# Queries and keys of batches 2 and 3 turned by the DMA crossbar instead of TensorE

## The chip, the cores and the metric

One core of one Trainium2 chip. The metric is the device time of one execution in microseconds (us); a profile of one execution gives its span, which is some 1.8 us shorter. Most executions agree within about 1%, but some are a few per cent longer ("slow": over 1.5% above the fastest of the same kernel). A ratio is the mean time of one kernel's fast runs over that of the kernel before in the same rounds on the same chip, with a 95% interval; it is therefore not quite the ratio of the medians quoted beside it.

## The reference, cut to what matters

```python
# q, k, v: (4 batches, 8 heads, 768 rows, 64), values 0.1 * normal
scores = q @ k.T / 8                       # keys kept: the 8 global rows, and 96 local ones
scores = where(keep, scores - slope[h] * dist, -1e9)
x = softmax(scores) @ v                    # heads side by side: (4, 768, 512)
x1, x2, x3 = split(x @ w_proj, 3)          # "gate" matmuls
y = x1 * irfft(rfft(x2) * rfft(filter)) * x3
out = y @ w_out                            # "output" matmuls, f32
```

Scores contract over the 64 values of a head, so TensorE needs queries and keys with these 64 on the partitions: each tile of 128 rows x 512 (8 heads x 64) has to be turned before its scores.

## The kernel before: the parts that the change touches

The program is first a graph of operations with estimated costs. A list scheduler lays it on the five engines' queues; its ranks come from a table of numbers (`NUDGES`) that was found by search for exactly this graph. Each queue is then run in order by the hardware.

Loads from HBM are issued by GpSimd (f32 to f16 on the way, 256-byte pieces in SBUF), a tile of 128 rows at a time, into one buffer `qn` (6 tiles) and one buffer `kn` (7 tiles), used by every batch in turn. A tile can be loaded again only when it has been turned. A key tile has 120 rows of its own and 8 rows for the global keys.

```python
    def transposes(self, what, t, src, cols):
        ...
            for i in range(4):                       # 4 x (128 x 128), f16, into one PSUM bank
                nc.tensor.transpose(b.f16()[:, P * i:P * i + P],
                                    src[:, 2 * i:2 * i + 2, :], self.ident)
        ...
        g.op("AV", ...copy of the bank into QT or KT, by ScalarE or VectorE...)
        if what == "k" and t == 0:                   # global key columns of all 7 tiles, by VectorE
            self.copy("V", kv[:, :, :, 0:NG], kv[:, :, 0:1, NG:2 * NG].to_broadcast([P, 4, 7, NG]))

    def load_global(self, vt, s):                    # global value rows, SBUF to SBUF, on SyncE
        for c, (t, n) in enumerate(((0, 2), (2, 5))):
            self.load("S", vt[0:NG, t:t + n], vt[NG:2 * NG, 0:1].to_broadcast(...), ...)

    def attention(self, b):                          # for b > 0, three groups c of rows
        for c in range(3):
            for t in ([0, 1, 2], [3, 4], [5])[c]:
                self.transposes("q", t, self.qn[:, t], P * t)
            for t in self.GRP[c]:                    # key tiles of the group: 0,1 / 2,3 / 4,5,6
                self.transposes("k", t, self.kn[:, t], P * t)
            for i in range(4):
                self.scores(i, c, ...)
            ...values, small transposes; gate matmuls of group c - 1...

    def fill(self, out):                             # idle matmuls where TensorE is planned to wait
        ...
            gap = o.start - at - 2.2 * (at < BEGIN + 1.0)
            n = int((gap - 0.1) / self.BUSY)
```

## Time and profile before

The median is 175.86 us. The profile is of another execution, of 177.28 us, and has a span of 175.5 us. What bounds it is read in the prediction below. Here are only lines of the page on its DMA queues. The first is a queue (packets, MB, packet time as a share of the 16 engines' span); the others are kinds of DMA with their size and the median us from issue to landing.

```profile
q1 hardware_dynamic: 4424, 7.30, 11.5%
...
vn<-in_v_dram POOLq DMA_DIRECT2D x28, 120.0 KB, 6.1
kn<-in_k_dram POOLq DMA_DIRECT2D x21, 120.0 KB, 6.0
qn<-in_q_dram POOLq DMA_DIRECT2D x18, 128.0 KB, 6.7
```

q1 is the queue of SyncE: 11.5% of 175.5 us is 20.2 us of the 16 engines, for the output, two loads of the first batch and the small copies. The loads are in another queue, q0.

| of the kernel before | us |
|---|---|
| first gate matmul starts | 27.0 |
| last scores of batch 1 / first of batch 2 / first of batch 3 | 60.6 / 72.5 / 117.3 |
| last output matmul starts | 171.4 |

These landmarks are start times in TensorE's timeline. From the first gate to the last output matmul TensorE works almost without a hole.

### The profile page before, as it was taken

The numbers are of one execution on the slowest core, as the hardware profiler recorded it, in microseconds if no ns is written. First come the engines' busy times: TensorE is split into PE (matmuls) and PEld (weight loads), VectorE is DVE, ScalarE is ACT, GpSimd is POOL, SyncE is SP. The second block draws the span as 40 slices with busy tenths as digits, with TensorE's granted clock in tenths as the row PEclk, the third lists the DMA queues.
The fourth block names the chain that finished last, engine by engine and source line by source line (L and its number), as shares of the span: only waits on it lengthen the run. The fifth ranks groups of instructions, "written<-read, shape, count | busy, mean of one in ns | idle before, by whom it ended". The sixth has DMA issues, their size and how long they took to land.

```text
span 175.5 us, 4566 instructions
## 1 busy us (share of the span) xinstructions
PE 166.9 (95%) x1768; PEld 104.3 (59%) x1768; DVE 157.0 (89%) x368; ACT 152.6 (87%) x304; POOL 75.3 (43%) x97
## 2 busy tenths in 40 slices
PE   7799999999899799999999999999999999999991
PEld 2357777665457567575446669754556674547540
DVE  6669778999999769999999998999899999998960
ACT  8879989999999778999997977999799897968751
POOL 7999986298997699998040300000000000000000
PEclk9999999999999999999999999999999999999998
DMA  5999999999999999999999900000710000043145
GB/s 177 148 145 134 146 200 209 166 152 138 135 166 159 132 141 142 146 144 149 66 63 344 70 4 4 0 0 0 294 70 4 0 2 4 0 159 140 60 166 197
DMA packets 79853, 20.06 MB, mean 114 GB/s; under 512 B 70528, under 2 KB 76888, under 8 KB 79832
## 3 DMA queue, kind: packets, MB, share of 16 engines
q0 software_dynamic: 75408, 12.47, 107.2%
q1 hardware_dynamic: 4424, 7.30, 11.5%
q8 instruction: 14, 0.23, 0.5%
q14 instruction: 7, 0.06, 0.1%
HBM read 25.69 MB, written 6.29 MB: 182 GB/s over the span
## 4 chain that ended last, share of the span: by engine, by line
PE 64%; DVE 14%; DMA 9%; POOL 5%; ACT 5%; issue 2%; ACTq 0%; POOLq 0%; DVEq 0%
PE bank L1098 19%; PE bank L1215 12%; DMA qn<-in_q_dram 9%; PE bank L1159 6%; PE bank L1181 4%; PE bank L1015 4%; PE bank L924 4%; PE bank L938 3%; PE bank L1020 3%; PE bank L975 3%; PE bank L1060 3%; ACT E L990 3%; POOL kn L583 2%; POOL vn L583 2%; PE bank L630 2%
## 5 line engine op out<-in xcount | busy, mean ns | idle before, releaser
L1098 PE MATMUL bank<-xT,w 128*128 128x384 f16 x256 | 45.6, 326 | 0.0
L990 ACT ACTIVATE E<-bank 128x864 f16<-128x864 f32 x48 | 41.0, 923 | 1.7 <-PE bank L975 1.3
L1098 PEld LDWEIGHTS <-w 128*128 128x128 f16 x256 | 23.9, 98 | 15.8 <-issue 0.8
L583 POOL DMA_DIRECT2D kn<-in_k_dram x24 | 21.6, 908 | 14.0 <-PE bank L938 6.6
L583 POOL DMA_DIRECT2D vn<-in_v_dram x29 | 26.2, 922 | 2.0 <-DMA w<-in_moe_w_proj_dram 1.6
L1215 PE MATMUL bank<-wo,y 128*128 128x512 f16 (+1 forms) x100 | 21.8, 371 | 0.1
L583 POOL DMA_DIRECT2D qn<-in_q_dram x21 | 18.6, 892 | 5.9 <-PE bank L755 3.2
L997 DVE TENSOR_TENSOR E<-E,mask 128x864 f16<-128x864 f16 x36 | 20.9, 597 | 0.1
L1039 DVE TENSOR_TENSOR xn<-bank,rc 128x512 f16<-128x512 f32 (+1 forms) x24 | 18.5, 775 | 0.4
L571 ACT ACTIVATE ot<-bank 128x512 f32<-128x512 f32 (+1 forms) x23 | 13.1, 606 | 5.1 <-PE bank L1215 5.0
L1108 ACT CAST g<-bank 128x384 f16<-128x384 f32 x32 | 15.7, 494 | 1.4 <-PE bank L1098 1.2
L1015 PEld LDWEIGHTS <-E 128*128 128x128 f16 x224 | 14.1, 97 | 3.6 <-DVE E L997 1.1
L571 ACT ACTIVATE ab<-bank 128x512 f16<-128x512 f32 x23 | 14.3, 633 | 2.2 <-PE bank L1159 2.0
L1215 PEld LDWEIGHTS <-y 128*128 128x128 f16 x100 | 9.5, 98 | 10.7 <-DVE y L1257 0.8
L1015 PE MATMUL bank<-vn,E 128*128 128x65 f16 x224 | 15.8, 194 | 0.0
L571 ACT ACTIVATE x<-bank 128x384 f16<-128x384 f32 x28 | 13.8, 507 | 2.3 <-PE bank L1098 1.8
L1020 PE MATMUL bank<-vn,E 128*128 128x65 f16 x192 | 15.4, 193 | 0.0
L975 PE MATMUL bank<-QT,KT 64*128 64x216 f16 (+2 forms) x224 | 15.0, 241 | 0.1
L1020 PEld LDWEIGHTS <-E 128*128 128x128 f16 x192 | 13.3, 97 | 0.4
L567 ACT CAST X<-bank 128x512 f16<-128x512 f32 x21 | 12.3, 643 | 0.0
L975 PEld LDWEIGHTS <-KT 64*128 64x128 f16 x224 | 8.3, 94 | 5.6 <-issue 3.0
L924 PE MATMUL bank<-ab,fwd 128*128 128x512 f16 x40 | 11.4, 379 | 0.0
(144 smaller groups left out, 358.2 us busy)
## 6 DMA issues: line engine op xcount, KB each, us to landing
out_dram<-ot SPq DMA_DIRECT2D x23, 256.0 KB
vn<-in_v_dram POOLq DMA_DIRECT2D x28, 120.0 KB, 6.1
kn<-in_k_dram POOLq DMA_DIRECT2D x21, 120.0 KB, 6.0
qn<-in_q_dram POOLq DMA_DIRECT2D x18, 128.0 KB, 6.7
w<-in_moe_w_proj_dram POOLq DMA_DIRECT2D x4, 256.0 KB, 7.3
g<-in_moe_filter_fft_dram POOLq DMA_DIRECT2D x1, 768.0 KB, 12.5
qn<-in_q_dram POOLq DMA_DIRECT2D x3, 192.0 KB, 5.0
kn<-in_k_dram POOLq DMA_DIRECT2D x3, 192.0 KB, 5.1
```

What stands on the lines that cost most here:

```text
L571: self.nc.scalar.mul(out, in_, c)
L583: return self.g.op(eng, 0.57 + 0.00035 * nbytes[0] if eng == "G" else 0.5, lambda _: e.dma_start(dst, src), w=w, r=r, nbytes=nbytes, name= ...
L924: self.nc.tensor.matmul(b.f32(), self.fwd[:, f], src(i, t), start=(n == 0), stop=(n == len(terms) - 1))
L975: nc.tensor.matmul(bs[hh].f32()[:, off:off + w], self.KT[hs, hp, P * m:P * m + P], self.QT[hs, hp, KL * m:KL * m + w], start=(off == 0 and ...
L990: g.op("A", act(864), lambda _: nc.scalar.activation(eo, bs[0].two()[:, :, 0:432].rearrange("p h (m w) -> p h m w", m=2), Act.Exp, scale=s ...
L997: g.op("V", dve(864, 2), lambda _: nc.vector.tensor_mul(eo, eo, mk), r=[("E", hp, gi), ("mask", hp)], w=[("E", hp, gi)], name="masked")
L1015: nc.tensor.matmul(o[:, n, hh], ef[:, at:at + P], vt[:, t, 2 * hp + hh, :], start=first, stop=(t == 0), skip_group_check=True)
L1020: nc.tensor.matmul(o[:, n, hh], ef[:, at:at + P], vt[:, t - 1, 2 * hp + hh, :], start=False, stop=True, skip_group_check=True)
L1039: nc.vector.tensor_mul(to, o[:, :, :, 0:D], rc.to_broadcast([P, 2, 2 * nt, D]))
L1098: nc.tensor.matmul(bk.f32()[:, 0:h], self.w[:, c, o + P * j:o + P * j + P], self.xT[:, c, h * s:h * s + h], start=(c == 0), stop=(c == 3))
L1108: g.op("A", act(h), lambda _: nc.scalar.copy(x3, pts[1].f32()[:, 0:h]), use=[pts[1]], w=[ko], name="x3")
L1215: nc.tensor.matmul(bk.f32()[:, 0:n], y[:, c, P * t:P * t + P], self.wo[:, c, cs], start=(c == 0), stop=(c == 3))
```

## The change

The intent: TensorE is the fullest engine, so the 104 transposes of batches 2 and 3, and the copies that follow them on ScalarE and VectorE, go to the DMA crossbar, whose result lands in QT and KT directly. As the crossbar turns all 128 rows, the global key rows have to be in each tile beforehand: SyncE copies them within `kn`, once the tiles of batch 1 have been turned. Some idle matmuls more keep TensorE's clock up in front.

```diff
+    CROSS = frozenset((b, w, t) for b in (2, 3) for w in "qk" for t in range(7))
...
+    def turned(self, b, what, t, src, cols):
+        if (b, what, t) not in self.CROSS:
+            self.transposes(what, t, src, cols)
+            return
+        dst = (self.QT if what == "q" else self.KT)[:, :, cols:cols + P]
+        keys = [("kng", min(t // 2, 1))] if what == "k" else []
+        self.g.op("S", 1.3, lambda _: self.nc.sync.dma_start_transpose(
+            out=dst, in_=src.rearrange("p h d -> p (h d)")), r=[(what + "n", t)] + keys,
+            w=[(what.upper() + "T", t)], nbytes=(512, 650), name=what + "T")
...
-    def load_global(self, vt, s):
+    def load_global(self, tile, key, *r):            # now for kn of batches 2 and 3 too
...
-                gap = o.start - at - 2.2 * (at < BEGIN + 1.0)
+                gap = o.start - at - 2.0 * (at < BEGIN + 1.0)
...
-    NUDGES = (...)      # 2112 numbers, now 2064, all new: the whole order is searched again
+    NUDGES = (...)
-    FAVOUR = 0.1
+    FAVOUR = 0.0
```

(The estimate for one load of the first batch was raised as well, 1536 to 1990.)

## The prediction

> **What bounds the kernel now.** I read the page's busy shares and forty slices first, to see which engine is full and where.
>
> ```profile
> PE 166.9 (95%) x1768; PEld 104.3 (59%) x1768; DVE 157.0 (89%) x368; ACT 152.6 (87%) x304; POOL 75.3 (43%) x97
> ...
> PE   7799999999899799999999999999999999999991
> ...
> DVE  6669778999999769999999998999899999998960
> ACT  8879989999999778999997977999799897968751
> ...
> DMA  5999999999999999999999900000710000043145
> ```
>
> The span is 175.5 us, so one slice is 4.4 us. TensorE is full from slice 14 (about 60 us) to the last; VectorE and ScalarE are nearly full as well, so three engines are close together, TensorE ahead. The DMA engines are 9 tenths full until about 88 us and almost empty afterwards: batches 2 and 3 are loaded in the first half. I then asked for the windows, to see whether "full" has holes.
>
> ```profile
> 27.00:60.00 33.00, 31.18 (x320) 19.41 (x317) 30.57 (x74) 31.00 (x58) 24.16 (x28) 1.00 2.33 158
> 112.00:171.00 59.00, 59.00 (x487) 33.96 (x486) 55.91 (x118) 50.62 (x99) 0.00 (x0) 1.00 0.17 66
> 27.00:171.00 144.00, 141.87 (x1379) 87.83 (x1376) 135.96 (x296) 128.11 (x244) 50.59 (x57) 1.00 1.11 103
> ```
>
> The columns are the window, its length, then busy us of PE, PEld, DVE, ACT and POOL, then clock, DMA share and GB/s. From the first gate matmuls (27 us) to the last output matmul (171 us) TensorE is idle for only 144.00 - 141.87 = 2.1 us, 1.8 of them before 60 us, and the clock is full. Thus work taken off TensorE after 27 us should come off the end nearly one for one, if nothing takes its place.
>
> Busy time of a matmul here includes its latency (219 ns for a transpose), so I take paces from the chain of waits, where the pieces are disjoint:
>
> ```profile
> PE 64%; DVE 14%; DMA 9%; POOL 5%; ACT 5%; issue 2%; ACTq 0%; POOLq 0%; DVEq 0%
> ...
> 49.13 9.36 DMA qn<-in_q_dram
> 58.54 0.40 PE bank L938 x4
> ...
> 109.61 1.12 PE bank L938 x20
> ...
> 111.06 0.89 PE bank L938 x16
> ```
>
> L938 is the transpose to be replaced: 0.89/16 and 1.12/20 us are 56 ns each. The chain also shows that at 58.5 us TensorE reached the first query tile of batch 2 before it had landed, 9.36 us after its issue. The waits confirm who suffers:
>
> ```profile
> POOL kn L583 <- PE bank L938: 6.6, 2, 5.0
> ...
> PE bank L938 <- DMA qn<-in_q_dram: 1.0, 1, 1.0
> ```
>
> 1.0 us of TensorE idleness is that tile; the load queue in turn waits 6.6 us for TensorE to release key tiles, which costs nothing by itself.
>
> **What the Trainium skill says.** "VectorE: DVE Perf Modes", section The three transpose paths, gives a 128x128 bf16 transpose as 390 ns on TensorE and 1309 ns through the DMA crossbar. The trace has 219 ns of latency and 56 ns of pace on TensorE, so the page's figure is an isolated latency; no crossbar transfer is in this trace. "Advanced Engine Details and Errata", section X-Bar Transpose (TRN2), expects 350-400 GB/s and calls transposing DMAs as fast as plain ones; it also wants one transposing stream at a time, and here all are on the SyncE queue. "DMA: Bandwidth & Descriptors", section Issuing engines are not separate DMA queues, says that all queues share the same 16 engines: a transpose then competes with the loads that fill the DMA row until 88 us. "TensorE: Matmul & The Clock Gate", Part 1, says that the array runs at half clock until it has been busy for about 3.4 us. The trace agrees:
>
> ```profile
> 1.19 4.88 PE L563 MATMUL bank<-idle 128*128 128x512 f16 x11 [1.19 <-DVE idle L677]
> ```
>
> Eleven idle matmuls took 4.88 us, 0.44 us each, where a 512-column output matmul runs at 0.216 us later (12 in 2.59 us on the chain).
>
> **The change part by part.** The set of crossed tiles is 6 query and 7 key tiles of batches 2 and 3, 26 tiles of 128x512.
>
> 1. Removed from TensorE: 26 x 4 = 104 transposes. The instruction order confirms it: kn 84 to 28, qn 72 to 24. 104 x 56 ns = 5.8 us, all after 58 us, all in the stretch where TensorE has no holes: on the path.
>
> 2. Removed from ScalarE and VectorE: 26 copies out of PSUM and 2 copies of global key columns. The order drops 21 from ScalarE and 5 from VectorE. At 0.60 us (medians 0.599 for QT, 0.592 for KT) that is 12.6 us of ScalarE; at 0.42 us for QT and 0.40 for KT, 2.0 us of VectorE, and 2 x 0.26 = 0.5 us for the key columns. Other copies are dealt out anew between the two. They run beside TensorE, so I credit no extra time; they do make it likelier that TensorE's predecessors are ready, notably from 65 to 88 us, where the chain runs along VectorE.
>
> 3. Added on SyncE: 26 transposing DMAs of 128 KB, and 4 small copies of global key rows. At the page's 350 GB/s a tile is an estimated 0.37 us, at 1309 ns per 128x128 block run one after another 5.2 us. The truth lies between, and decides the case. These DMAs are in order in one queue, so I counted what the order leaves for them. Between the last scores of batch 1 and the first of batch 2 TensorE now has 32 gate matmuls (16 in 2.60 us), 48 value matmuls (24 fill the 0.8 us between gates and filter at 63.4 us), 16 of the inverse transform (32 in 2.6 us from 141.5 us), 12 small transposes (6 in 0.34) and 4 of the filter (at most 0.9): 9.7 us. Query tile 3 can only be overwritten after those last scores, and key tiles 0 and 1 stand behind it in the queue: three transposes in 9.7 us. By the same count the third group of scores comes 22 us after, with ten transposes. Taking 4 us for one transfer's fixed part and landing (an estimate from the shortest load, 3.8 us), the queue may take (9.7 - 4)/3 = 1.9 and (22 - 4)/10 = 1.8 us a tile before TensorE stalls. In batch 3 the first keys are issued well before the end of batch 2's scores and the remaining groups come 12 us and more after the first, so it has more room.
>
> 4. Moved: the 8 global rows of each key tile go into kn by SyncE copies rather than into KT by VectorE; they wait for the last transposes of batch 1 (done before its last scores) and add one landing (a few us) ahead of the key transposes of batch 2, while query tile 3 is being waited for. Hidden, I think.
>
> 5. Idle matmuls: 25 instead of 16. Twelve instead of eleven in front, at 0.44 us, end about 6.4 us; the first data arrive at 7.09 us, so it is free. Seven stand between the first batch's parts, where TensorE waits for loads or ScalarE. One comes in the middle (0.22 us at most). I count +0.2 us.
>
> 6. The early stage is laid anew too: ScalarE gets more of the first batch's QT and KT copies (about 2.4 us more, net of a cast given to VectorE), with its exponentials on the chain there. That may move the first gate by a microsecond either way; I count +0.5.
>
> Sum: -5.8 (transposes) - 0.5 (half of the 1.0 us wait for the query tile; the rest comes back as a wait for its turned form) + 0.2 + 0.5 + 0.5 (small stalls behind the crossbar) = -5.1 us. From 175.86 this gives 170.8 us.
>
> **The rivals.** (a) The crossbar is slow or starved: with 2.5 us a tile the queue would overrun by (2.5 - 1.8) x 10 = 7 us in batch 2 and eat the gain: 175 to 178 us. For it speak the full DMA row at that time and landing times of the plain query loads of 3.8/6.6/12.2 us (shortest, median, longest); against it that the transfers come from SBUF, wide, and with a second, nearly empty queue. (b) VectorE or ScalarE becomes the bound: they were 89% and 87% busy against 95%. After the change I get about 152, 139 and 161 us for VectorE, ScalarE and TensorE, so TensorE stays first, but VectorE at 9 tenths could hold back a microsecond or two in the stretch from 65 to 88 us, giving 171 to 173 us. (c) Loads of batch 3 come earlier, because a tile is released by a landing rather than by TensorE's turn, or later, as the transposes take DMA time from them; TensorE has gates and convolution of batch 2 to do meanwhile, so I expect neither to show: 0 us. (d) The lighter copying removes hidden bubbles too, and all of the early waits go: 168 to 169 us.
>
> **Range and chances.** Centre 170.8. The 8-in-10 range runs from 168.0 (rival d) to 174.3 (half of rival a). Faster by over 2% means under 172.3: the sum leaves 1.5 us for that, so rivals (b) or a third of (a) already spoil it. I give faster 0.70, within 2% 0.25, slower 0.05.
>
> **What would show it right or wrong.** L938 should have 52 instructions instead of 156, about 161 us busy on TensorE plus the idle matmuls, and no hole over 1 us after 60 us. In the waits, TensorE's scores (L975's successor) should wait for a transposing DMA less than 1.5 us in total; if it is several, rival (a) holds, and the landing time of the transposes should be well over 4 us. The first gate should stay within 1 us of 27.2 us; if the time moves there, step 6 was wrong. If TensorE is idle waiting for VectorE or ScalarE between 65 and 110 us, rival (b) holds. The stretch from 112 us to the end contains none of the removed work: its content should only shift earlier, by about 5 us.

## The result, and the profile after

The kernel after took 183.98 us (median of four runs, 181.94 to 187.76) against 176.16 us before: a ratio of 1.038 [1.026, 1.050]. It is slower. Two of its four runs count as slow, among them the profiled one (184.75 us). So its sizes below are those of a run about 2 us longer than the fast ones; the same stalls are in later runs of the same order, fast ones among them.

From the page of the kernel after: busy times, then the forty slices of TensorE, of its granted clock and of the DMA engines.

```profile
PE 164.4 (90%) x1673; PEld 100.2 (55%) x1673; DVE 150.7 (82%) x358; ACT 145.6 (80%) x286; POOL 75.4 (41%) x97
...
PE   7999998999999895099999993899999999999991
...
PEclk9999999999999999569999999699999999999999
DMA  5999999999999999999999999990006200024135
```

TensorE has less to do than before (1673 matmuls for 1768), but two holes that were not there: slices 16 to 17 and 25, about 71 to 78 and 112 to 115 us. After each hole its clock is low for a slice or two. The DMA row was 9 tenths full to slice 23 before (101 us; the prediction's "about 88 us" misread it); now it is full to slice 27, 123 us. TensorE's timeline names the holes (start, length, operation, and in brackets the idle time ahead and what ended it):

```profile
78.04 1.26 PE L984 MATMUL bank<-QT,KT 64*128 64x216 f16 x12 [6.79 <-DMA KT<-kn]
79.24 2.94 PE L1107 MATMUL bank<-xT,w 128*128 128x384 f16 x12
...
115.11 0.54 PE L984 MATMUL bank<-QT,KT 64*128 64x216 f16 x4 [3.51 <-DMA KT<-kn]
```

The first scores of batch 2 waited 6.8 us and those of batch 3 3.5 us for key tiles from the crossbar, 10.3 us in all. The twelve gates after the first hole took 2.94 us; at the full clock twelve take 2.11 us in the kernel before. The page's DMA part shows why the keys were late:

```profile
q1 hardware_dynamic: 18712, 10.83, 31.6%
...
vn<-in_v_dram POOLq DMA_DIRECT2D x28, 120.0 KB, 10.1
kn<-in_k_dram POOLq DMA_DIRECT2D x21, 120.0 KB, 10.1
qn<-in_q_dram POOLq DMA_DIRECT2D x18, 128.0 KB, 8.6
...
KT<-kn SPq DMA_TRANSPOSE x14, 9.0
QT<-qn SPq DMA_TRANSPOSE x12, 7.6
```

A turned tile lands 7.6 to 9.0 us after its issue, and the plain loads are slower as well (10 us for 6). SyncE's queue now takes 31.6% of 183.0 us, 57.8 us of the 16 engines, 37.6 more than before; over 26 tiles that is 1.4 us a tile (with the small key copies in it). This is engine time, averaged over the 16, and not how long a tile holds the queue up. For that the packet records are needed. They do not name the tile; here and below they are dealt out to the tiles in the order of the queue, 512 packets each. The 13 tiles of batch 2 were on their way through SyncE's queue from 58.05 to 90.75 us, one behind the other and with the small copies among them: 2.5 us a tile. The median tile had its first packet 5.5 us after its issue, and its last 1.85 us after the first. (The last packet comes before the landing that a waiting engine sees, here by about 1 us.) The chain of waits of the kernel after (start, length, what) carries both delays:

```profile
69.33 8.66 DMA KT<-kn
...
96.61 8.00 DMA kn<-kn
104.68 1.67 SPq L956
106.40 8.66 DMA KT<-kn
```

In batch 2 the chain runs through one key tile, issued at 69.33. In batch 3 it runs through two landings in series: the copy of the global key rows, issued at 96.61, and then the key tile that had to wait for it.

### The profile page after: what moved, and what is told of

The parts are those of the page before. It is cut to its first block, busy times and chain, and to the rows that moved or that the text cites. A ratio compares the mean times of both kernels' runs of the same rounds, so it can differ in the third digit from the quotient of the medians.

```text
span 183.0 us, 4411 instructions
## 1 busy us (share of the span) xinstructions
PE 164.4 (90%) x1673; PEld 100.2 (55%) x1673; DVE 150.7 (82%) x358; ACT 145.6 (80%) x286; POOL 75.4 (41%) x97
## 3 DMA queue, kind: packets, MB, share of 16 engines
q1 hardware_dynamic: 18712, 10.83, 31.6%
## 4 chain that ended last, share of the span: by engine, by line
PE 50%; DVE 18%; DMA 14%; ACT 12%; issue 2%; SPq 2%; ACTq 0%
PE bank L1107 15%; DMA KT<-kn 9%; PE bank L1168 9%; PE bank L1224 8%; DMA kn<-kn 4%; PE bank L1190 4%; PE bank L984 4%; ACT E L999 4%; DVE xn L1048 2%; PE bank L921 2%; DVE E L1006 2%; PE bank L1024 2%; ACT slope L569 2%; PE bank L1069 2%; SPq L956 2%
## 5 line engine op out<-in xcount | busy, mean ns | idle before, releaser
L1107 PE MATMUL bank<-xT,w 128*128 128x384 f16 x256 | 47.3, 332 | 0.0
L984 PE MATMUL bank<-QT,KT 64*128 64x216 f16 (+2 forms) x224 | 16.2, 257 | 10.3 <-DMA KT<-kn 10.3
L1224 PE MATMUL bank<-wo,y 128*128 128x512 f16 (+1 forms) x100 | 22.4, 371 | 0.0
L1048 DVE TENSOR_TENSOR xn<-bank,rc 128x512 f16<-128x512 f32 (+1 forms) x24 | 18.4, 768 | 0.2
L984 PEld LDWEIGHTS <-KT 64*128 64x128 f16 x224 | 8.8, 98 | 16.8 <-DMA KT<-kn 10.6
L569 ACT ACTIVATE ot<-bank 128x512 f32<-128x512 f32 (+1 forms) x24 | 14.0, 608 | 4.8 <-PE bank L1224 4.7
L569 ACT ACTIVATE ab<-bank 128x512 f16<-128x512 f32 x23 | 13.8, 612 | 3.3 <-PE bank L1168 3.3
L569 ACT ACTIVATE x<-bank 128x384 f16<-128x384 f32 x25 | 12.3, 505 | 4.2 <-PE bank L1107 3.8
L565 ACT CAST eo<-bank 128x384 f16<-128x384 f32 x30 | 13.2, 490 | 0.9 <-PE bank L1193 0.7
L1069 PE MATMUL bank<-ident,xn 128*128 128x128 f16 x112 | 10.6, 224 | 1.6 <-DVE xn L1048 1.5
```

The costliest lines, as they stand in the source:

```text
L569: self.nc.scalar.mul(out, in_, c)
L984: nc.tensor.matmul(bs[hh].f32()[:, off:off + w], self.KT[hs, hp, P * m:P * m + P], self.QT[hs, hp, KL * m:KL * m + w], start=(off == 0 and ...
L1048: nc.vector.tensor_mul(to, o[:, :, :, 0:D], rc.to_broadcast([P, 2, 2 * nt, D]))
L1107: nc.tensor.matmul(bk.f32()[:, 0:h], self.w[:, c, o + P * j:o + P * j + P], self.xT[:, c, h * s:h * s + h], start=(c == 0), stop=(c == 3))
L1224: nc.tensor.matmul(bk.f32()[:, 0:n], y[:, c, P * t:P * t + P], self.wo[:, c, cs], start=(c == 0), stop=(c == 3))
```

## The experiments

Expectations are quoted. The main theory was that crossed tiles and loads get in each other's way on the DMA engines ("contention"). Its rivals: the traffic of more bytes alone, the crossing being slow by itself, the order of the queue, the new early stage, the clock, and VectorE as the bound.

### Plain copies in place of the crossing (x1_plain)

```diff
-        self.nc.sync.dma_start_transpose(out=dst, in_=src.rearrange("p h d -> p (h d)"))
+        self.nc.sync.dma_start(dst, src.rearrange("p (i h) d -> p i (h d)", i=4))
```

> The changed kernel with each of its 26 transposing DMAs replaced by a plain copy of the same tile into the same place on the same queue: same bytes, same waits, same order on every engine, no crossbar; the result is wrong on purpose. Theory 'traffic' (any 128 KB transfer is slow beside the loads of batches 2 and 3, which share the 16 DMA engines): copies land after 6 to 9 us, TensorE still waits 8 to 11 us for key tiles, time 180 to 184 us. Theory 'crossbar beside loads' (it is the transposing that mixes badly with the loads): copies land after 3 to 5 us, the waits fall under 3 us, time 171 to 175 us.

The bytes are right and the numbers are not, on purpose (the comparison passed it nevertheless. The reference shows why: put into it in this wrong order, the queries and keys of batches 2 and 3 change the output by 1.5%, and queries and keys of zero in all batches by 1.4%. So a passed comparison does not show that crossed tiles are turned rightly, in this run or in any other). Median 174.62 us (172.78 to 176.45, two of the four runs slow), ratio 0.979 [0.972, 0.986]. TensorE's timeline of this kernel (a slow run) at the same place:

```profile
73.39 0.73 PE L984 MATMUL bank<-QT,KT 64*128 64x216 f16 x12 [2.47 <-DMA KT<-kn]
```

Copies of the same bytes in the same order still make TensorE wait, but 2.5 us instead of 6.8, and in batch 3 not at all. So the traffic alone has a small price, and the transposing form the greater one. Neither expectation came true whole: waits and time are those of "crossbar beside loads", but the copies landed as late as "traffic" said.

```profile
KT<-kn SPq DMA_DIRECT2D x14, 128.0 KB, 7.8
QT<-qn SPq DMA_DIRECT2D x12, 128.0 KB, 7.5
```

Where does the difference come from, if a copy takes nearly as long to land (9.0 and 7.6 us in the kernel after)? In SyncE's timeline a copy's issue took 0.6 to 0.7 us where the queue was free, a transpose's 1.2 to 2.4. In the packet records of both traces, key tile 1 landed 6.7 us after its issue here and 7.3 us there, hardly a difference; but it was issued at 65.15 us here and at 69.33 there. The six tiles up to this one, with the small copies among them, set off at the same time and were through at 71.84 us here (from 58.21) and at 76.68 there (from 58.05): the queue as a whole is faster with copies. Both hold the same 512 packets of 256 bytes. The queue's share is 24.4% of 173.9 us, 42.4 us, which by the same subtraction of 20.2 us makes 0.85 us a tile against 1.4.

### Light loads (x2_light), and their control (x12_before_light)

```diff
# in load_rows and load_q: batches 2 and 3 load one head of eight (wrong result on purpose)
-                  src[b, :, lo:hi, :].rearrange("h p d -> p h d"), ...
+                  src[b, 0:n, lo:hi, :].rearrange("h p d -> p h d"), ...      # n = 1 if b > 1 else 8
```

> The changed kernel with the loads of queries, keys and values of batches 2 and 3 cut to one head of eight (same DMAs and waits, an eighth of the packets; result wrong on purpose), so that the transposes run nearly alone. Theories 'traffic' and 'crossbar beside loads': a transpose takes 0.6 us on the DMA engines as the last four of the changed kernel do, lands after 2.5 to 4 us, TensorE's waits for key tiles fall from 10.3 us under 2 us, time 170 to 174 us. Rival 'inherent latency' (a transposing DMA needs some 7 to 8 us whatever runs beside it): landing stays at 7 to 9 us, waits 8 us and more, time 180 us and more.

> The kernel before, with the loads of batches 2 and 3 cut to one head of eight, as in x2_light (wrong result on purpose; the instructions of every engine stay the same). It is the control that x2_light lacked. Theory (contention): the kernel before hardly waits for loads of batches 2 and 3, only 1.0 us for one query tile and part of 1.8 us of holes before 60 us, so light loads give it at most 1 to 2 us: ratio to before 0.990 to 1.000, 174.5 to 176 us; then about 3 of the 4.5 us that x2_light was ahead are the worth of turning by the crossbar when nothing else uses the DMA engines. Rival (the light loads alone made x2_light fast, and the crossed transposes are worth nothing even without contention, as x9_sorted_b3 hints for batch 3): ratio 0.970 to 0.978, 171 to 172.5 us.

Both give a relative error of 0.96. The order of every engine is unchanged.

| | full loads | light loads | what the loads cost |
|---|---|---|---|
| before | 1.000 | 0.9917 [0.985, 0.999] | 0.8% |
| after | 1.038 [1.026, 1.050] | 0.9714 [0.967, 0.976] | 6.9% |

(The last column is one ratio over the other.) The medians are 175.73 us for the kernel before with light loads and 171.79 us for the kernel after. Light loads hardly help the kernel before, and they turn the kernel after from the slower into the faster one. Without them next to it, crossing is worth 1 - 0.9714/0.9917 = 2.0%, about 3.6 us (by the two intervals, some 1 to 3%). The page of x2_light says how fast the crossbar is without loads in its way:

```profile
q1 hardware_dynamic: 18712, 10.83, 22.6%
```

22.6% of 170.5 us is 38.5 us, so 18.4/26 = 0.7 us a tile: half of the 1.4 us in the kernel after, for the same packets. By the packet records a tile takes 0.77 us from its first to its last packet and its last packet comes 2.0 us after its issue (median; the landings of the DMA list are 2.4 us for keys and 2.9 for queries, to be held against 9.0 and 7.6); the issue is still 1.2 us.

As x2_light has the order of the kernel after, the stages can be set against each other:

| us, from TensorE's timelines | before | before, light | after | after, light |
|---|---|---|---|---|
| first gate | 27.02 | 27.48 | 28.77 | 28.89 |
| last scores of batch 1 | 60.55 | 59.84 | 61.77 | 62.13 |
| first scores of batch 2 | 72.48 | 71.77 | 78.04 | 71.55 |
| first scores of batch 3 | 117.30 | 115.90 | 115.11 | 103.86 |
| last output matmul | 171.44 | 170.04 | 178.90 | 166.42 |
| first gate to last output | 144.42 | 142.56 | 150.13 | 137.53 |

This is the account of the result. With light loads the change takes 142.56 - 137.53 = 5.0 us off the stretch from the first gate on, and starts it 1.4 us later. Full loads lengthen that stretch by 12.6 us in the kernel after (150.13 - 137.53), and by 1.9 us before. So -5.0 for the change, +10.7 for contention (12.6 - 1.9) and +1.75 for the start (28.77 - 27.02) make +7.45 us, and the last output matmul is indeed 7.46 us later (178.90 - 171.44). Of the 12.6 us, 10.3 are the two waits. These are single profiles, that of the kernel after of a slow run; the ratios of fast runs give nearly the same size, 1.069/1.008 or 6.0%, some 10.5 us, for contention.

### Only batch 3, or batch 2 put back, with the order laid anew (x3_before_b3, x4_after_b3)

```diff
# x3: the kernel before, its NUDGES, and the crossing with
+    CROSS = frozenset((3, w, t) for w in "qk" for t in range(7))
# x4: the same set in the kernel after, its NUDGES
```

> The kernel before with batch 3 alone turned by the crossbar (52 transposes and 13 copies less), all other ranks of the plan as before. TensorE saves 52 x 56 ns = 2.9 us. Theory 'traffic or crossbar beside loads': the transposes of batch 3 come when few loads are left, so they land after 3 to 6 us and TensorE waits under 2 us for them: 173 to 176 us. Rival 'inherent latency': landing 7 to 9 us against the 5 to 6 that the plan leaves, waits of 3 us and more, 176 to 180 us.

> The changed kernel with batch 2 turned on TensorE again, batch 3 still by the crossbar, all other ranks of the plan as in the changed kernel. The stall of 6.8 us before batch 2's first scores must go. TensorE does 52 transposes more (2.9 us). All theories with the stall as the cause: 175 to 179 us. If the loss of the changed kernel came mainly from its new early stage or its new order instead: 181 us and more.

181.04 us, ratio 1.025 [1.020, 1.030], and 197.26 us, ratio 1.103 [1.095, 1.110]. Neither tells the theories apart. The numbers of `NUDGES` were found for one graph; with another graph they give a worse order (x3 had 46 idle matmuls, and no wait for a turned key; x4 stalled in many places).

### Batch 3 crossed with the order of the kernel before held (x5, x6, x7, x9)

After laying, each pair of transpose and copy is replaced by one transposing DMA at the copy's place, on SyncE. x6 and x7 cross four and eight late tiles of batch 2 as well; x9 is x5 with the tiles sorted by need and the global key rows first.

```diff
+        return self.program(self.crossed(self.fill(self.lay())))   # x5: batch 3 substituted
# x6, x7: + (2, "q", 5), (2, "k", 4..6)  and  + (2, "q", 3..5), (2, "k", 2..6)
# x9, in crossed():
+            mine.sort(key=lambda m: (max(0, (m[2] - 1) // 2), m[1] == "k", m[2]))
```

> The kernel before with its order held on every engine, except that the 52 transposes and 13 copies of batch 3 are left out and 13 transposing DMAs (with two copies of global key rows before them) stand on the SyncE queue instead; nothing is planned anew, so the mistake of x3 (a plan laid anew with ranks made for another graph) can't recur. By the theory that a transpose is quick once the loads are through (0.8 us on the DMA engines, landing 2 us after issue), batch 3's tiles are all turned between about 97 and 123 us, TensorE waits under 1 us for them and saves 52 x 56 ns = 2.9 us: 172 to 174.5 us against 176.5. If a crossbar transpose costs time whatever lies beside it: 176 us and more.

> As x5_held_b3, and also key tiles 4 to 6 and query tile 5 of batch 2 by the crossbar: these are needed at 98 us and have landed by 75, so the contention with the last loads has some 20 us to hide in. 16 transposes more off TensorE: 0.9 us less than x5, 171 to 174 us, if hidden; 1 us or more above x5 if the slowed loads of batch 3 matter.

> As x6, and also query tiles 3, 4 and key tiles 2, 3 of batch 2, which run fully beside the loads (60 to 80 us) and are needed by 83 us. By the contention theory each takes some 2 us and lands after 7 to 8 us: just in time or 1 to 4 us late, so 171 to 177 us, and the landing time of these first tiles must be several times that of batch 3's.

> As x5_held_b3 (the order of before held, batch 3 alone by the crossbar), but the 13 transposes stand in the SyncE queue in the order in which the scores need them, and both copies of global key rows before them; in x5 the tile that the first scores waited for stood last, and at 1.2 us an issue thirteen tiles take 16 us. By the traces the loads are through by about 102 us, so each lands 2 us after its issue, the last by 118 us; batch 3's first scores come at 115 us and need the first five. TensorE's waits for QT and KT under 1 us: 172.5 to 174.5 us against 176.5. If a crossbar transpose still can't be hidden where it has the DMA engines to itself: 176 us and more.

x5: 186.79 us, ratio 1.058 [1.050, 1.066]. The tiles landed in 2.0 us, with no loads left, but thirteen issues of 1.2 to 1.3 us each stood in series, and the query tile needed first stood last:

```profile
PE bank L1015 <- DMA QT<-qn: 9.5, 1, 9.5
```

The order of the queue alone can lose 9.5 us. x6 and x7, 201.85 us (1.140 [1.131, 1.149]) and 198.99 us (1.125 [1.118, 1.133]), carried the same fault and a further one: in x6 TensorE waited 13.2 us for the copy of the global key rows, which stood behind other copies in the queue. Their times are artefacts of my substitution and say nothing for or against contention. In the packet records of x7, the first tile of batch 2, beside the loads, took 5.4 us to its last packet and those of batch 3 took 2.0 us, which goes the way that its expectation said.

x9, in an order by need, took 176.88 us, ratio 1.003 [0.998, 1.008]: nothing gained, where I had expected 2 to 4 us. In its trace TensorE waits for no turned tile at all. Windows of the stretch where the transposes had been, first before and then x9 (columns as in the prediction: busy time of PE, PEld, DVE, ACT, POOL, clock, DMA):

```profile
100.00:112.00 12.00, 12.00 (x174) 9.96 (x172) 11.41 (x28) 9.75 (x21) 0.00 (x0) 1.00 0.11 9
```

```profile
100.00:112.00 12.00, 10.46 (x129) 7.75 (x128) 11.56 (x26) 7.30 (x15) 0.00 (x0) 1.00 0.77 107
...
109.65 0.51 PE L1106 MATMUL bank<-ident,xn 128*128 128x128 f16 x6 [0.99 <-DVE xn L1085]
110.70 4.06 PE L1144 MATMUL bank<-xT,w 128*128 128x384 f16 x24 [0.55 <-DVE xT L601]
```

Fewer matmuls (129 for 174), but VectorE is as full as before, and TensorE now waits for it, 1.5 us in two pieces. I read this so: in this order part of the removed transposes had merely filled TensorE beside a chain that VectorE paces. No run tests it. In the order of the kernel after this is not so: x2_light got its 5.0 us. Of these two orders, taking transposes away paid only in the one that was laid for it.

### Keys first (x8_keys_first)

```diff
+        for o in [o for o in s if o.name == "kT"][:2]:      # keys 0 and 1 of batch 2
+            s.remove(o)
+            s.insert(s.index([x for x in s if x.name == "qT"][2]), o)
```

> The changed kernel with one swap in the SyncE queue: key tiles 0 and 1 of batch 2 are issued ahead of query tile 2, the value rows and query tile 3, not behind them; all other engines' orders are the same. If the 6.8 us stall before batch 2's first scores is the in-order queue (four slow issues and a wait for batch 1's last scores standing ahead of the keys), it falls to 1 to 4 us, some of it coming back at the second group of scores: 177 to 181 us against 183. If only the shared DMA engines set it, the stall stays at 5 us and more and the time at 182 us and more.

182.79 us, ratio 1.031 [1.021, 1.040]: within the noise of the kernel after. The first wait fell from 6.8 to 6.4 us only. The keys now stood at the head of the queue and waited there for the copy of the global key rows. In SyncE's timeline of x8:

```profile
57.94 1.56 SPq L585 DMA_DIRECT2D kn<-kn  x2
65.10 3.57 SPq L960 DMA_TRANSPOSE KT<-kn  x2
68.77 1.23 SPq L960 DMA_TRANSPOSE QT<-qn  x1
```

The two copies were issued from 57.94 us on and the keys only at 65.1. By the packet records key tile 1 then had its last packet at 73.6 us, 3.1 us earlier than in the kernel after, but the third query tile, now behind it, at 77.1 instead of 69.9. The chain of waits of x8 runs through that query tile and no longer through a key:

```profile
68.77 9.20 DMA QT<-qn
```

The first scores need both, so a new place in the queue gains little: what counts is when all that they need is through.

### The idle matmuls (x10_one_idle, x11_warm)

```diff
# x10: the kernel before with
-                gap = o.start - at - 2.2 * (at < BEGIN + 1.0)
+                gap = o.start - at - 2.0 * (at < BEGIN + 1.0)
# x11: the kernel after with 20 idle matmuls ahead of the first scores of batch 2, 10 of batch 3
+                    n = {25: 20, 37: 10}.get(seen, n)
```

> The kernel before with only the third part of the change, the gap constant in front at 2.0 instead of 2.2, which gives one idle matmul more before the first data. I expect no difference: 176 to 177 us, within 0.5 us of before. If the cold clock of the first microseconds matters: 0.5 us faster or more.

> The changed kernel with 20 idle matmuls before batch 2's first scores and 10 before batch 3's, inside the two stalls of 6.8 and 3.5 us, which they don't lengthen (4.3 and 2.2 us). The stalls stay; only the clock stays warm. If the half clock after each stall costs what the matmul paces after it say (gates 0.24 for 0.16 us, about 1.5 us each time), the time falls by 1.5 to 3.5 us, to 180 to 181.5 us; if it is nothing, it stays at 182 to 184 us.

x10: 176.12 us, ratio 1.001 [0.997, 1.005]. The idle matmul in front is free, as predicted. x11: 183.22 us, ratio 1.036 [1.030, 1.043], no better than the kernel after within the noise. Its profile, of a fast run, shows the first hole filled and the gates behind it at full pace:

```profile
70.77 4.48 PE L564 MATMUL bank<-idle 128*128 128x512 f16 x20
76.89 0.73 PE L987 MATMUL bank<-QT,KT 64*128 64x216 f16 x12 [1.64 <-DMA KT<-kn]
77.55 2.12 PE L1110 MATMUL bank<-xT,w 128*128 128x384 f16 x12
```

The twelve gates took 2.12 us for 2.94, and still the end did not move by an amount that the runs can tell. So the low clock is for the most part a mark of the wait and not the cause of the loss; a share of about 1 us is below what two ratios with 0.6 and 1.2% of noise resolve, and is not excluded. (The idle matmuls for batch 3 did not help there: the trace still shows the low clock behind that wait.)

### Loads held back (x13_loads_wait, x14_more_wait)

Can the order of the loads save the change? A copy of 8 columns on GpSimd, out of key tile 1 of batch 2, stands in GpSimd's queue ahead of one load, so that it and all later ones are issued only when keys 0 and 1 have landed. In x13 that is the load of query tile 5, in x14 of key tile 2, four loads earlier (the expectation's "five" is a miscount). The result passes the comparison (for what that says, see x1) and every other order is held.

```diff
+        o.eng, o.fn, ..., o.name = "G", Plan.hold, ..., "hold"   # copy(held, KT[:, 0, 2 * P - 8:2 * P])
+        at = out.index([x for x in out if x.eng == "G" and x.name == "q5"][1])    # x14: load of kn 2
+        out.insert(at, o)
```

> The kernel after, its order held; only, a tiny GpSimd copy out of key tile 1 of batch 2 stands in front of the load of query tile 5 of batch 2, so that this load and all later ones are issued only when keys 0 and 1 have landed. Correct result. Theory (loads that are in flight beside the crossed tiles make them late): the loads issued from 62.7 us on are out of the way of query tile 3 and keys 0 and 1, the landing of these keys falls from 7 to 8 us to 3 to 5, and TensorE's first wait from 6.8 to 3 to 5 us; as the held loads come some 6 us later, part comes back in the later groups or in batch 3: 179 to 183.5 us in all, ratio to before 1.015 to 1.04. Rival (the crossing is slow by itself in this place, or the order alone is to blame): the landing stays at 7 us or more, the wait at 6 us or more, and the time is over 184 us because the loads come later.

> As x13_loads_wait, with the held point five loads earlier, in front of key tile 2 of batch 2. Theory (loads in flight): keys 0 and 1 now cross almost alone, landing 2 to 3 us after issue, and TensorE's first wait is under 2 us; but some ten tiles of loads start 10 us later than in the kernel after, and the DMA engines were full until 120 us there, so the loss moves to the later groups of batch 2 and to batch 3: 180 to 186 us, and it tells whether order can save the change or whether the DMA engines' time itself is short. Rival (crossing slow by itself): landing over 5 us, wait over 5 us.

x13: 179.45 us (178.70 to 180.11), ratio 1.017 [1.010, 1.024]. x14: 184.83 us (182.76 to 186.08), ratio 1.037 [1.027, 1.046]. The packet records of the four traces, for key tile 1 of batch 2 (us; the last column counts load packets that started between its first and its last packet):

```
                 issued   first packet   last packet   from issue   load packets between
after            69.33       75.30          76.68         7.3            615
x13_loads_wait   66.62       71.07          71.66         5.0              0
x14_more_wait    66.68       67.87          68.64         2.0              0
x2_light         66.91       68.09          68.87         2.0              0
```

The loads are all that was changed between the first three, and the tile's landing follows them. In x13 no load was left beside the tile itself; what remained was the queue, as the query tile two places ahead of it had taken 3.5 us beside the last loads. Key tile 0 tells the same (8.1, 5.8 and 2.6 us in the first three). TensorE's timelines follow, in x13 first and then in x14:

```profile
73.16 0.73 PE L991 MATMUL bank<-QT,KT 64*128 64x216 f16 x12 [1.80 <-DMA KT<-kn]
87.58 0.25 PE L991 MATMUL bank<-QT,KT 64*128 64x168 f16 x2 [0.62 <-DMA KT<-kn]
88.88 0.20 PE L991 MATMUL bank<-QT,KT 64*128 64x48 f16 x2 [1.05 <-DMA KT<-kn]
```

```profile
83.41 0.72 PE L991 MATMUL bank<-QT,KT 64*128 64x216 f16 x6 [4.63 <-DMA QT<-qn]
```

In x13 the first wait falls from 6.8 to 1.8 us, new ones of 0.6 and 1.1 us appear in later groups, the first scores of batch 3 still wait 2.9 us, and about 4 us of the loss are won back. In x14 the first wait is gone (scores at 70.62 us), but the loads held back return as a wait of 4.6 us for a query tile and of 3.1 us for key tiles, and the time is that of the kernel after. Less waiting at one place has to be paid for by loads at another. Neither beats the kernel before; no version that I tried with all loads and true transposes does.

## Why the prediction was wrong

It said 170.8 us and gave "slower" one chance in twenty. Signs that it had named for being wrong came true: scores waited 10.3 us for transposing DMAs (it allowed 1.5), these landed well over 4 us after their issue, and the first gate moved by 1.75 us (it allowed 1). By its own steps:

1. *Transposes off TensorE, -5.8 us on the path.* About right for this order: 5.0 us with light loads, steps 1 and 2 together. x9 shows that the premise ("TensorE has no holes, so its work comes off the end") is not safe by itself: in the order before, half of the transposes came off and the end stayed, with VectorE as the pacer (rival b).
2. *Copies off ScalarE and VectorE, no credit.* VectorE fell about as told (157.0 to 150.7 us, for 152), ScalarE by half of what was told (152.6 to 145.6, for 139). That no credit was given was right.
3. *The crossing, +0.5 us for "small stalls behind the crossbar".* **This step failed**, in each number of its count of the queue. It reckoned with three transposes in the queue before the first scores of batch 2. In the kernel after, six tiles and four small copies stood there, and they were through at 76.7 us, while the last scores of batch 1 had begun at 61.8. It allowed 1.8 to 1.9 us a tile; the 13 tiles of batch 2 took 2.5 us each. It allowed "4 us for one transfer's fixed part and landing", taken from the shortest load before; the landing was 7.6 to 9.0 us, most of it (5.5 us in the median) gone before the tile's first packet, behind loads and the tiles ahead. And the issue, of which the step said nothing, took 1.2 to 2.4 us each. The first wait alone was 6.8 us, and the term came to about +10.7 us in place of +0.5. I had read the full DMA row as rival (a)'s argument and set it aside because the queue was "nearly empty". It was so before the change; with 26 tiles in it, and the engines behind it full of loads, it was not.
   "Batch 3 ... has more room" failed likewise: its loads, held up by the crossing of batch 2, were still under way at 110 us, and its first scores waited 3.5 us.
4. *Global key rows, "Hidden, I think".* Wrong: the copies landed as late as everything else. They are 8.0 us of the chain of batch 3, in batch 2 the keys were held up by them until 67.1 us, and in x8 they were what the keys of batch 2 waited for.
5. *Idle matmuls, +0.2 us.* The one in front is harmless, by x10; the other eight were not tested alone. ("The trace agrees" on the clock holds for the half pace and not for the 3.4 us: in that trace the idle matmuls at 8.51 us, 7.3 us after the first, are still at half pace, 0.4 us apart.)
6. *The early stage, +0.5 us.* The sign was right; 1.4 to 1.75 us is what the first gate shows, 28.8 for 27.0 to 27.5 us, in every kernel with the new order. No run undid it alone.

Rival (a) was the right one, and even its pace, 2.5 us a tile, is what the queue shows. Its size, "175 to 178 us", was too small because it let the queue overrun only at the third group of scores, and not already at the first. Rival (c) was dismissed with "0 us"; the loads did come later, and that is part of what batch 3 lost.

Shown by the runs: the loss is the meeting of loads and crossed tiles on the DMA engines (x2_light with its control, x13, x14), and the transposing form is far dearer in it than a copy (x1). Not shown: how much of that is the longer issue and how much the slower passage, what makes a transposing tile hold the engines twice as long beside loads, and how an order searched for the loads and the crossing together would do.

## What to carry to other kernels

Here, work moved from a full engine to the DMA engines gained 2% where these had time and lost 4% where they had none: look at the DMA row at the moment of the move, and take the landing time of the transfers that run there, not the shortest one in the trace. Where a tile is waited for, count every landing in series (here global rows, then keys) and every transfer ahead of it in the same queue, with its issue. To learn what a transfer costs by itself and what beside others, thin out the others, and do the same to the kernel before as a control.

## What the Trainium skill lacked or had wrong

- "Advanced Engine Details and Errata", section X-Bar Transpose (TRN2): "TRN2 transpose DMAs are as fast as regular DMAs". Of the engines' time that was nearly so with no load packet beside them (by the packet records 0.60 to 0.64 us for most tiles in x2_light, 0.57 for the last plain copies of x1), and not so beside loads: 1.4 us against 0.85 for a plain copy. The issue took 1.2 us or more against 0.6. Swapping the one for the other moved the kernel by about 6% (ratios 1.038 and 0.979). From first to last packet a tile took 0.77 us alone (131,072 bytes in that time are 170 GB/s), and 0.48 us at best, where it had waited in the queue (x11, 273 GB/s); the page expects 350-400.
- "VectorE: DVE Perf Modes", section The three transpose paths, gives 1309 ns for a 128x128 block by the crossbar. Four blocks in one DMA landed 2.4 to 2.9 us after the issue with light loads and 7.6 to 9.0 us beside full ones (medians); the page does not say under what load its figure holds.
- "DMA: Bandwidth & Descriptors", section Rules for kernel authors, says of the crossbar that "A transpose next to ordinary DMAs needs nothing". No run here shows it for the results, as the comparison does not see queries and keys (x1); for the time there is a word missing, as the neighbours decided whether the change won 2% or lost 4%. Its section Issuing engines are not separate DMA queues held: a second queue gave no relief (7.3 us to a key tile's last packet with loads in the other queue, 2.0 without).
